# A fused attention, channel-mix and FFT-mix kernel: later output copies and stores, paired value tiles, a third place for weights, a second set of stage buffers, sums apart

## The chip, the cores and the metric

One core of one Trainium2 chip runs the whole program. The metric is the device time of one execution in microseconds (us), median of several runs. A time is also given for the profiled execution, whose trace is quoted below.

## What is computed

Three blocks follow each other: attention with a sigmoid in place of the softmax, a channel mix with token shift (squared ReLU and a sigmoid gate), and a block that adds the real part of a two-dimensional FFT, normalises and runs a two-layer network. All is float32; the kernel multiplies with fp32r operands split into a high and a low part, three matmuls for each product.

```python
# B, S, D = 4, 448, 768; 12 heads of 64
attn = 1 / (1 + exp(-(q @ k.T / 8 - log(S))));  x = attn @ v        # (B, S, D)
xk, xr = mix(x, mu_k), mix(x, mu_r)                                 # with the token before
k = maximum(xk @ w_k, 0);  v = (k * k) @ w_v                        # D -> 1024 -> D
x = sigmoid(xr @ w_r) * v
u = x + real(fft(fft(x, axis=1), axis=2))
un = (u - mean(u)) / sqrt(var(u) + 1e-6)
out = u + maximum(un @ w_ch1, 0) @ w_ch2                            # D -> 3072 -> D
```

## The kernel before

**How the order comes about.** The program is written out by a planner (`Order`, line 136). Each piece of work is a Python generator that yields the planned time at which it wants to go on. `need` (L162) waits until a named mark is set and its planned time has come, `issued` (L169) only until it is set. The planner adds up costs for each engine and for the transfers; an instruction is emitted when its generator comes to it. On the chip each engine then runs its instructions strictly in that order. Matmuls go through a list (`feed`) one at a time. `dma` (L270) puts a transfer on SyncE's queue (SP); with `add=True` it is an accumulation into memory on GpSimd's queue (POOL), and with a third argument `G` a plain transfer on that queue. A delay or a wait in one generator therefore changes where its instructions stand among all others.

**Stages on TensorE.** Attention and keys up to 257 us, receptance (`r`) up to 343, values (`v`, with the FFT's matmuls `pa`, `qa`, `pq` between them) up to 493, the plain part of the first network layer (`f`) up to 562, the visits (`f_X`, `f_Y`, `f_W`) up to 822, the second layer (`m`) to the end. A 448-column matmul takes 0.20 us on the average when nothing waits.

**Values** (`values`, L847). For each of the four batches b six output tiles e are made, each of 8 terms f with 3 matmuls. Term f reads `k2` of (b, f), which `load_k2` (L759) loads into a ring of 12 places: a place is free when the last tile (e = 5) of the batch that used it has read it. `r_t` comes through `load_r` on POOL's queue, and `val_done` (L833) multiplies a tile out of PSUM on VectorE into `x2`, which has three buffers for four batches (`new_x2`, L839, waits for `centre` of batch b - 3). `centre` (L1040) subtracts the mean; for b = 0 it also stores the result to `c_d` on SP. `squares` (L1076) squares the first two batches on ScalarE and stores or accumulates them to `vs_d` on POOL. `rows0` (L1222) forms the sums for the visits after `centre` 1, and `centre` of batch 2 is put in order behind it.

**Visits** (`VISITS`, L131; `visits`, L1318; `visit`, L1377). The first layer is done by a seven-product scheme. Sixteen visits go over groups g of 256 columns: v = 0 to 3 with the first pair of batches (p = 0), v = 4 to 7 with both, v = 8 to 15 with the second (p = 1). A visit for one pair has 63 matmuls. `visit_loads` (L1298) loads two weight chunks for each visit into places `w0`, `w1` (later also `k0` to `k2`), `visits` forms the seven split blocks of them (`blk`), and `after` copies results out of PSUM: `w7` and `u2` (`tmp`, L1381) and stage tiles (`stage`, L1355), all sent to `h_d` on POOL. For p = 0 they lie in buffers `s0`, `s1` and `hst`, for p = 1 in `sum_u`, `sum_v`, `rsb` and `sq`, one of each.

**Second layer** (`second`, L1438). Seven products m for each pair p, 108 matmuls each, three row tiles e side by side. The results gather in three tiles of tag `x2`. For p = 0 `after0` (L1464) scales them, and `store` (L1451) accumulates each into `u_d` and then copies it from there to the output, both on POOL. For p = 1 `after` (L1497) adds onto `u_d` that was loaded, and `store` writes the output by SP.

Of the kernel before, what the change touches and what calls it, by code (L numbers as in the profile page):

```python
# [12 lines left out]
F32 = mybir.dt.float32  # L13
# [8 lines left out]
B, H, S, DH = 4, 12, 448, 64  # L22
D = H * DH
NP = H // 2
DFF = 1024
NF = DFF // 128
# [14 lines left out]
PL, JO, EARLY = 4, 8, 8  # L41
# [239 lines left out]
def build(tc, ap):  # L281
    nc = tc.nc
    V, G = nc.vector, nc.gpsimd
    o = Order(nc)
# [73 lines left out]
    u_d = [dram.tile([128, KD, S], F32, name=f"u_d{b}") for b in range(B)]  # L358
    w0_d = [dram.tile([128, 2, D], F32, name=f"w0_d{f}") for f in range(2 * PL)]
    c_d = dram.tile([128, KD, S], F32, name="c_d")  # L360
# [447 lines left out]
    np_ = pool(s_r, "norm", 1, "right")  # L808
# [38 lines left out]
    def values():  # L847
        for b in range(B):
            o.spawn(new_x2(b))
            for es in ((0,), (1,), (2,), (3,), (4, 5)):  # L850
                while len(o.feed) > 6:
                    yield o.now + 0.1
                ts = [(e, []) for e in es]
                for i in range(0, NF, NF // len(es)):
                    for e, ps in ts:
                        cs = slice(128 * e, 128 * e + 128)

                        def pair(t, b=b, cs=cs):
                            return wvh[:, t, cs], wvl[:, t, cs], k2_t[b, t][:, 0], k2_t[b, t][:, 1]

                        ks = {t: ("k2", b, t) for t in range(NF)}
                        yield from o.tile(
                            partial(bank, f"v_{b}_{e}"),
                            NF,
                            pair,
                            partial(val_done, b, e),
                            ("val", b, e),
                            ks,
                            ps,
                            range(i, i + NF // len(es)),  # L870
                        )
            o.spawn(spectrum(b))
        yield from o.issued(("x2", B - 1, KD - 1))
        o.at["values"] = o.now
# [165 lines left out]
    def centre(b, ps):  # L1040
        u = x2_t[b]
        mean_of = ps[:, 0:S]
        if b < 2:
            o.spawn(squares(b), o.now + 1.0)
        if b == 2:
            yield from o.issued(("centre", 1))
            mean = np_.tile([128, S], F32, tag="rsb", name="mean_2", bufs=1)
            yield o.act(mean, mean_of, AF.Copy, scale=1.0 / D)
        for i in range(3):
            xx = u[:, 2 * i : 2 * i + 2]  # L1050
            yield from o.need(("u_d", b, i))
            for h in range(2):
                if b == 2:
                    t = o.tt(V, xx[:, h], xx[:, h], mean, ALU.subtract)
                else:
                    t = o.stt(xx[:, h], mean_of, -1.0 / D, xx[:, h], ALU.mult, ALU.add)
                o.at["c", b, 2 * i + h] = t
            yield t
            if b == 0:
                o.at["c_d", i] = o.dma(c_d[:, 2 * i : 2 * i + 2], xx) + 2.0  # L1060
            if b < 2:
                continue
            if b > 2 and i == 0:
                yield from o.issued(("scaled", b - 1))
            sq = ft(b, "sq", [128, 2, S], pl=np_)
            yield o.act(sq, xx, AF.Square)
            add_up(b, "v", i, sq)
        if b < 2:
            return
        yield from scale(b)  # L1070
        for i in range(KD):
            t = o.tt(V, u[:, i], u[:, i], rs_t[b], ALU.mult)
            yield t
        o.at["centre", b] = o.now

    def squares(b):  # L1076
        u, landed = x2_t[b], 0.0
        if b > 0:
            yield from o.issued(("centre", 0))
        for i in range(3):  # L1080
            yield from o.need(("c", b, 2 * i + 1))
            if i == 1:
                ts = [np_.tile([128, S], F32, tag=tag, name=f"sq_{b}_{tag}", bufs=1) for tag in ("sum_v", "rsb")]
            else:
                sq = ft(b, "sq", [128, 2, S], pl=np_)
                ts = [sq[:, 0], sq[:, 1]]
            for h, t in enumerate(ts):
                done = o.act(t, u[:, 2 * i + h], AF.Square)
            yield max(done, landed)
            for h, t in enumerate(ts):  # L1090
                landed = o.dma(vs_d[b][:, h], t, G, add=i > 0) + 2.0
            yield landed
        o.at["centre", b] = o.now
# [116 lines left out]
    al = pool(s_l, "al", 1, "left")  # L1210
# [81 lines left out]
    wt_t, place_t = {}, {}  # L1292
    for v, (g, ps) in enumerate(VISITS):
        for j in range(2):
            i = 2 * (v - NG + PL) + j
            place_t[v, j] = ("w0", "w1", "k0", "k1", "k2")[i % 5] if i >= 0 else f"w{j}"

    def visit_loads():  # L1298
        last = {}
        for v, (g, _) in enumerate(VISITS):  # L1300
            for j in range(2):
                place = place_t[v, j]
                if place in last:
                    yield from o.need(("wt free", *last[place]))
                elif place[0] == "k":
                    yield from o.need(("prod", LAST0))
                last[place] = (v, j)
                yield from o.need(("w_d", 2 * g + j))
                name = f"a_{v}_{j}"
                if place in ("w0", "w1"):  # L1310
                    t = al.tile([128, D], F32, tag=place, name=name, bufs=1)
                else:
                    t = ring(23 + 4 * int(place[1]), [128, D], F32, name)
                o.at["wt", v, j] = o.dma(t, w_d[2 * g + j])
                wt_t[v, j] = t
                yield o.now + 0.1
# [36 lines left out]
        yield o.now  # L1353

    def stage(p, q, g):  # L1355
        if p == 0:
            return al.tile([128, S], F32, tag="hst", name=f"h_{p}_{q}_{g}", bufs=2)
        return np_.tile([128, S], F32, tag=("rsb", "sq")[q], name=f"h_{p}_{q}_{g}", bufs=1)

# [3 lines left out]
    def network():  # L1363
# [13 lines left out]
        def visit(v):  # L1377
            g, ps = VISITS[v]
            bk, tm = {}, {}

            def tmp(nm, p):  # L1381
                if p == 0:
                    t = al.tile([128, S], F32, tag={"u2": "s0", "w7": "s1"}[nm], name=f"{nm}_{v}", bufs=1)
                else:
                    t = np_.tile([128, S], F32, tag={"u2": "sum_u", "w7": "sum_v"}[nm], name=f"{nm}_{v}_1", bufs=1)
                tm[nm, p] = t
                return t
# [48 lines left out]
        chain, out = {}, {}  # L1436

        def second(p):  # L1438
# [12 lines left out]
            def store(nm, e, t):  # L1451
                yield t
                b, k = 2 * p + int(nm[1]) - 1, 3 * (int(nm[0]) - 1) + e
                dst = ap["out"][k, :, S * b : S * b + S]
                if p > 0:
                    o.dma(dst, out[p, nm][:, e])
                else:
                    o.dma(u_d[b][:, k], out[p, nm][:, e], add=True)
                    o.dma(dst, u_d[b][:, k], G)

            def add(nm, e, x):
                return o.tt(V, out[p, nm][:, e], out[p, nm][:, e], x, ALU.add)
# [34 lines left out]
            def after(m, e, ps):  # L1497
                if m == 0:
                    if e == 0:
                        tiles("t")  # L1500
                    o.at["tc", p, e] = o.act(out[p, "t"][:, e], ps)
                elif m == 1:
                    if e == 0:
                        tiles("22", "11")
                    yield from o.need(("res", p, "22"))
                    o.at["v", p, e] = add("22", e, ps)
                elif m == 2:
                    yield from store("11", e, add("11", e, ps))
                elif m == 3:
                    if e == 0:  # L1510
                        tiles("12", "21")
                    yield from o.need(("res", p, "12"))
                    o.at["w", p, e] = add("12", e, ps)
                elif m == 4:
                    o.at["z", p, e] = add("22", e, ps)
                elif m == 5:
                    t = out[p, "t"][:, e]
                    yield o.tt(V, t, t, ps, ALU.add)
                    t1, t2 = add("12", e, t), add("22", e, t)
                    o.at["y", p, e] = add("21", e, t)  # L1520
                    yield from store("12", e, t1)
                    yield from store("22", e, t2)
                else:
                    yield from store("21", e, add("21", e, ps))
                yield o.now
# [312 lines left out]
```

## Time and profile before

| | us |
|---|---|
| median of 3 runs (1136.02 to 1138.82) | 1136.56 |
| the profiled execution | 1138.76 |
| its span, first to last instruction | 1137.0 |
| TensorE busy in it | 1120.8 (99%) |
| VectorE busy | 804.3 (71%) |
| ScalarE busy | 649.7 (57%) |
| mean granted clock of TensorE | 0.994 of full speed |

The profile gives the busy time of each engine, the waits, and for any stretch the granted clock. A matmul that runs at half clock is busy twice as long, so a stretch has two losses: the idle time, and its length times what the granted clock lacks to 1.00.

### The profile page before, as it was taken

Reading aid. Unit: us, or ns where it says so; the run is one execution under the profiler, and the core shown is the slowest. Engines: PE = TensorE matmul, PEld = TensorE weight load, DVE = VectorE, ACT = ScalarE, POOL = GpSimd, SP = SyncE. Lnnn points to the kernel's source line nnn. Section 1 sums busy time; section 2 is a strip of 40 time slices with the busy share of each in tenths; the row PEclk is TensorE's granted clock in tenths of the full one; section 3 lists DMA queues with packets and bytes.
Section 4 is the critical chain, followed back from the end, with each engine's and each line's share of the span. In section 5 each row is a group of like instructions: output and inputs, shape, how many; then the busy total and the mean of one; then the engine's idle time right before and its main releaser. Section 6 shows DMA issues by size and latency. Waiting matters only on the chain.

```text
span 1137.0 us, 16897 instructions
## 1 busy us (share of the span) xinstructions
PE 1120.8 (99%) x5908; PEld 977.2 (86%) x5908; DVE 804.3 (71%) x1292; ACT 649.7 (57%) x1171; POOL 108.1 (10%) x205
## 2 busy tenths in 40 slices
PE   9999999999999999999999999999999999989998
PEld 3476676799999989999989999889999999979997
DVE  3876757666624668799787655777579799866887
ACT  6788777766632333354676666767655444444442
POOL 0000000100001011200111112111100100120000
PEclk9999999999999999999999999999999999989999
DMA  7765789768839798855968888989885648974432
GB/s 241 241 232 204 236 315 351 260 234 277 315 133 308 292 324 258 266 154 210 307 220 290 279 289 286 376 296 324 290 335 185 162 155 286 335 200 156 160 99 86
DMA packets 108597, 283.33 MB, mean 249 GB/s; under 512 B 13600, under 2 KB 44512, under 8 KB 108384
## 3 DMA queue, kind: packets, MB, share of 16 engines
q1 hardware_dynamic: 94176, 234.17, 60.5%
q0 software_dynamic: 14048, 47.63, 13.0%
q8 instruction: 46, 0.75, 0.3%
q10 hardware_dynamic: 288, 0.46, 0.1%
q14 instruction: 39, 0.32, 0.1%
HBM read 185.72 MB, written 99.23 MB: 251 GB/s over the span
## 4 chain that ended last, share of the span: by engine, by line
PE 66%; issue 19%; DMA 5%; DVE 4%; POOL 4%; ACT 2%; POOLq 0%; SPq 0%; ACTq 0%; DVEq 0%
PE m L213 20%; PE k L213 9%; PE v L213 9%; PE r L213 8%; PE av L213 6%; PE sc L213 4%; POOL h_d L274 3%; PE f_Y L213 3%; DMA u_d<-out 2%; PE f_W L213 2%; PE f_X L213 2%; PE pq L213 1%; PE sc_c L213 1%; DMA k<-k_d 1%; DVE r L248 1%
## 5 line engine op out<-in xcount | busy, mean ns | idle before, releaser
L213 PE MATMUL m<-hs,sw 128*128 128x448 f32 x1512 | 306.9, 365 | 3.8 <-ACT hs L265 2.9
L213 PEld LDWEIGHTS m<-hs,sw 128*128 128x128 f32 x1512 | 285.7, 189 | 24.6 <-ACT hs L265 3.3
L265 ACT CAST sw<-w 128x768 fp32r<-128x768 f32 x84 | 70.0, 834 | 80.3 <-PE m L213 49.1
L213 PE MATMUL v<-k,wvh 128*128 128x448 f32 x384 | 113.2, 369 | 1.9 <-DMA k<-k_d 1.9
L265 ACT CAST hs<-r 128x896 fp32r<-128x896 f32 x84 | 78.9, 940 | 60.9 <-DVE r L248 60.7
L248 DVE TENSOR_TENSOR sw<-w,sw 128x768 fp32r<-128x768 f32 x84 | 80.1, 954 | 34.0 <-ACT sw L265 33.8
L248 DVE TENSOR_TENSOR hs<-r,hs 128x896 fp32r<-128x896 f32 x84 | 91.3, 1087 | 16.7 <-ACT hs L265 16.4
L267 ACT ACTIVATE sg<-sc,bias_s 128x448 f32<-128x448 f32 x144 | 78.3, 651 | 12.6 <-PE sc L213 12.6
L213 PE MATMUL f_Y<-T,blk 128*128 128x448 f32 x360 | 77.8, 364 | 3.1 <-ACT u L265 3.1
L213 PE MATMUL f_W<-T,blk 128*128 128x448 f32 x360 | 78.4, 366 | 0.0
L213 PEld LDWEIGHTS v<-k,wvh 128*128 128x128 f32 x384 | 71.9, 189 | 7.5 <-DMA k<-k_d 2.6
L213 PEld LDWEIGHTS f_Y<-T,blk 128*128 128x128 f32 x360 | 67.5, 188 | 8.4 <-ACT u L265 3.9
L213 PEld LDWEIGHTS f_W<-T,blk 128*128 128x128 f32 x360 | 68.6, 191 | 4.8
L213 PE MATMUL k<-xkh,wkh 128*128 128x448 f32 x192 | 70.6, 368 | 0.9 <-ACT kt L267 0.9
L213 PE MATMUL k<-xkl,wkh 128*128 128x448 f32 x192 | 70.2, 366 | 0.0
L213 PE MATMUL k<-xkh,wkl 128*128 128x448 f32 x192 | 70.2, 365 | 0.0
L213 PE MATMUL v<-k,wvl 128*128 128x448 f32 x192 | 69.9, 364 | 0.0
L267 ACT ACTIVATE w_raw<-w_raw 128x384 f32<-128x384 f32 x80 | 44.2, 552 | 31.0 <-DMA w_raw<-in_w 31.0
L213 PE MATMUL av<-sg,v 128*64 128x448 f32 x288 | 57.2, 544 | 0.0
L265 ACT CAST blk<-a 128x384 fp32r<-128x384 f32 x80 | 40.5, 511 | 29.0 <-PE f_Y L213 9.8
L213 PE MATMUL f<-un,w1h 128*128 128x448 f32 x192 | 55.5, 364 | 0.0
L248 DVE TENSOR_TENSOR blk<-a,blk 128x384 fp32r<-128x384 f32 x80 | 43.5, 553 | 15.1 <-ACT blk L265 14.9
(227 smaller groups left out, 2146.3 us busy)
## 6 DMA issues: line engine op xcount, KB each, us to landing
w<-v_d SPq DMA_DIRECT2D x84, 384.0 KB, 3.4
w_raw<-in_w SPq DMA_DIRECT2D x80, 384.0 KB, 4.9
r<-h_d SPq DMA_DIRECT2D x48, 448.0 KB, 6.1
k_d<-kp SPq DMA_DIRECT2D x32, 448.0 KB, 3.7
k<-k_d SPq DMA_DIRECT2D x32, 448.0 KB, 6.1
h_d<-h POOLq DMA_DIRECT2D x56, 224.0 KB, 4.6
a<-w_d SPq DMA_DIRECT2D x32, 384.0 KB, 5.6
v_d<-w SPq DMA_DIRECT2D x48, 192.0 KB, 4.5
```

The lines of the kernel that those rows point to most:

```text
L213: self.nc.tensor.matmul(out, lhs, rhs, start=start, stop=stop, skip_group_check=skip)
L248: eng.tensor_tensor(out, a, c, op=op)
L265: self.nc.scalar.copy(out, a)
L267: self.nc.scalar.activation(out, a, fn, **kw)
L274: (eng or self.nc.sync).dma_start(out, src)
```

## The change

- `values`: tiles 0 and 1 of a batch now go in turns of four terms, as 4 and 5 do: half of tile 0, half of tile 1, the rest of 0, the rest of 1.
- `keep`: the stores of `c_d` wait until the last `k2` of batch 2 is planned to have landed; `squares` of batch b waits for the last `k2` of batch b + 2.
- `place_t`, `visit_loads`: the first four visits use the buffer `sq` as a third place for weights, once `centre` of the last batch is over.
- `stage`, `tmp`: odd visits with g below 8 (v = 9, 11, 13, 15) use the buffers of p = 0.
- `store` for p = 0: the copy to the output is issued 15 us after the planned landing of the accumulation. As it is one generator, what stands behind it in `after0` (the sum and the accumulation of "22" behind those of "12") comes later too.
- `after` for p = 1, m = 5: the sum that the last product needs goes first, the other two 2, 7 and 12 us later, one row tile after another.

```diff
@@ values
-            for es in ((0,), (1,), (2,), (3,), (4, 5)):
+            for es in ((0, 1), (2,), (3,), (4, 5)):
@@ centre
             if b == 0:
-                o.at["c_d", i] = o.dma(c_d[:, 2 * i : 2 * i + 2], xx) + 2.0
+                o.spawn(keep(i, xx))
@@
+    def keep(i, xx):
+        yield from o.need(("k2", 2, NF - 1))
+        o.at["c_d", i] = o.dma(c_d[:, 2 * i : 2 * i + 2], xx) + 2.0
+        yield o.now
+
     def squares(b):
         u, landed = x2_t[b], 0.0
+        yield from o.need(("k2", b + 2, NF - 1))
         if b > 0:
@@ place_t
-            place_t[v, j] = ("w0", "w1", "k0", "k1", "k2")[i % 5] if i >= 0 else f"w{j}"
+            k = 2 * v + j
+            place_t[v, j] = ("w0", "w1", "k0", "k1", "k2")[i % 5] if i >= 0 else ("w0", "w1", "w0", "w1", "sq", "w0", "w1", "sq")[k] if k < 8 else f"w{j}"
@@ visit_loads
                     yield from o.need(("wt free", *last[place]))
+                elif place == "sq":
+                    yield from o.need(("centre", B - 1))
...
+                if place == "sq":
+                    t = np_.tile([128, D], F32, tag="sq", name=name, bufs=1)
@@ stage
-        if p == 0:
+        if p == 0 or g < JO and g % 2:
@@ tmp
-                if p == 0:
-                    t = al.tile([128, S], F32, tag={"u2": "s0", "w7": "s1"}[nm], name=f"{nm}_{v}", bufs=1)
+                if p == 0 or g < JO and g % 2:
+                    t = al.tile([128, S], F32, tag={"u2": "s0", "w7": "s1"}[nm], name=f"{nm}_{v}_{p}", bufs=1)
@@ store
-                    o.dma(u_d[b][:, k], out[p, nm][:, e], add=True)
+                    t = o.dma(u_d[b][:, k], out[p, nm][:, e], add=True)
+                    yield t + 15.0
                     o.dma(dst, u_d[b][:, k], G)
@@ after, m == 5
-                    t1, t2 = add("12", e, t), add("22", e, t)
                     o.at["y", p, e] = add("21", e, t)
-                    yield from store("12", e, t1)
-                    yield from store("22", e, t2)
+                    yield o.now + 2.0 + 5.0 * e
+                    yield from store("12", e, add("12", e, t))
+                    yield from store("22", e, add("22", e, t))
```

## Rows read from the trace of the kernel before

**Rows 1.** Page, part 1: busy us of each engine, share, instructions.

```profile
PE 1120.8 (99%) x5908; PEld 977.2 (86%) x5908; DVE 804.3 (71%) x1292; ACT 649.7 (57%) x1171; POOL 108.1 (10%) x205
```

**Rows 2.** TensorE by stretch: width, busy (matmuls), granted clock, DMA share, GB/s.

```profile
415.00:424.00 9.00, 7.05 (x38) 0.81 1.03 416
...
573.00:575.00 2.00, 0.72 (x4) 1.00 0.61 249
...
615.00:616.00 1.00, 0.70 (x4) 1.00 1.16 408
...
736.00:738.00 2.00, 0.79 (x4) 1.00 1.04 408
...
750.00:758.00 8.00, 6.09 (x22) 0.79 0.59 173
...
999.00:1010.00 11.00, 7.68 (x22) 0.69 0.62 125
...
1122.00:1123.00 1.00, 0.53 (x3) 1.00 0.00 0
1123.00:1137.00 14.00, 10.45 (x53) 0.96 0.13 49
```

**Rows 3.** Waits of TensorE: what it waited for, total us, times, longest.

```profile
PE f_Y L213 <- ACT u L265: 3.1, 2, 1.9
PE m L213 <- ACT hs L265: 2.9, 1, 2.9
PE v L213 <- DMA k<-k_d: 1.9, 1, 1.9
PE f_Y L213 <- DVE w L248: 1.3, 1, 1.3
...
PE f_X L213 <- DVE blk L248: 0.3, 1, 0.3
```

**Rows 4.** Chain that ended last: start us, length us, what.

```profile
407.69 9.90 DMA k<-k_d
...
744.88 6.57 DMA h_d<-u
...
822.38 29.04 PE m L213 x145
...
979.30 7.55 DMA u_d<-out
...
996.10 4.26 DMA u_d<-out
```

**Rows 5.** TensorE in the value tiles alone, up to the wait at 415.6 us.

```profile
343.30:415.60 72.30, 65.19 (x309) 1.00 0.87 297
```

**Rows 6.** SyncE in order of time: start, length, instruction.

```profile
407.21 0.38 SPq L274 DMA_DIRECT2D c_d<-x  x1
```

**Rows 7.** GpSimd in order of time, with the idle time before in brackets.

```profile
406.05 1.08 POOL L274 DMA_DIRECT2D vs_d<-sq  x2 [3.42 <-ACT sq L267]
```

**Rows 8.** ScalarE in order of time, idle time before and its releaser in brackets.

```profile
736.74 0.53 ACT L265 COPY u<-f_Y 128x448 f32<-128x448 f32 x1 [0.40 <-DMA h_d<-u]
...
751.52 0.53 ACT L265 COPY u<-f_Y 128x448 f32<-128x448 f32 x1 [2.57 <-DMA h_d<-u]
...
1000.43 1.40 ACT L265 COPY out_t<-m 128x448 f32<-128x448 f32 x3 [10.53 <-DMA u_d<-out]
```

**Rows 9.** VectorE in order of time, likewise.

```profile
483.30 0.62 DVE L248 TENSOR_TENSOR x<-v,rv 128x448 f32<-128x448 f32 x1 [1.56 <-PE v L213]
...
569.79 0.56 DVE L248 TENSOR_TENSOR s<-a,a 128x384 f32<-128x384 f32 x1 [1.00 <-DMA a<-w_d]
...
1002.70 1.09 DVE L248 TENSOR_TENSOR hs<-r,hs 128x896 fp32r<-128x896 f32 x1 [11.81 <-ACT hs L265]
...
1113.44 3.29 DVE L248 TENSOR_TENSOR out<-out,out_t 128x448 f32<-128x448 f32 x6
```

**Rows 10.** All engines by stretch: width, busy PE, PEld, DVE, ACT, POOL, clock.

```profile
500.00:520.00 20.00, 20.00 (x131) 18.86 (x130) 19.00 (x41) 11.08 (x24) 2.72 (x5) 1.00 0.49 160
```

More of the change, by code (lines that the diff above doesn't have):

```diff
@@ L1309, in visit_loads @@
                 name = f"a_{v}_{j}"
-                if place in ("w0", "w1"):
+                if place == "sq":
+                    t = np_.tile([128, D], F32, tag="sq", name=name, bufs=1)
+                elif place in ("w0", "w1"):
                     t = al.tile([128, D], F32, tag=place, name=name, bufs=1)
```

## The prediction, made before the changed kernel was run

> **What bounds the kernel now.** I read the page first: TensorE is busy for 1120.8 of 1137.0 us [rows 1]. So no engine beside it matters on the average, and only two things can be won: the 16.2 us in which it idles, and the time in which it is busy at half clock. The second view is therefore TensorE by stretch, made so that each stretch holds one loss [rows 2]. The reader is to see that nearly all of the idle time after the first 343 us lies in seven short places and in the last 3.5 us, where the last results leave. In three of them the granted clock is below 1.00 as well: it fell to 1.2 GHz after the gap and came back to 2.4 GHz some us later. The loss of a stretch is its width less busy, plus its width times what the clock lacks:
>
> - 415 to 424: 1.95 idle, and 9 x 0.19 = 1.71 by the clock: 3.66 us.
> - 573 to 575: 1.28 us, clock full. 615 to 616: 0.30 us.
> - 736 to 738: 1.21 us. 750 to 758: 1.91 and 8 x 0.21 = 1.68: 3.59 us.
> - 999 to 1010: 3.32 and 11 x 0.31 = 3.41, together 6.73. Counted otherwise: 22 matmuls at 0.20 us would have been 4.4 of 11 us, so 6.6 us. I take 6.6.
> - 1122 to 1123: 0.47 us.
>
> The third view, TensorE's waits [rows 3], names who ended each: a load of k2 (415), the copy of u out of PSUM (736 and 750), the split of hs on ScalarE (1000), a sum on VectorE (573), a weight block (615). Each is then followed back in the chain and in the engines' own order [rows 4, 8, 9].
>
> **Part by part.**
>
> Values. TensorE had done 309 value matmuls when it stopped [rows 5]: 288 of batches 0 and 1 and 21 of tile 0 of batch 2. It stood before term 7, whose k2 was issued at 407.69 and landed 9.90 us later, at 417.6 [rows 4]. Batch 2 had begun 21 x 0.20 = 4.2 us before 415.55, at 411.35. With tiles 0 and 1 in turns, 12 + 12 + 9 = 33 matmuls stand before term 7, so it is wanted at 411.35 + 6.6 = 417.95, after it landed even if nothing else were changed, by a bare 0.35 us. Moving the stores helps more: the c_d store just ahead of that load [rows 6] is 448 KB and the two vs_d stores [rows 7] 448 KB; at the 416 GB/s of this stretch [rows 2] their 0.92 MB take 2.2 us. The load should land near 415.4, 2.5 us before it is wanted. That returns 3.66 us; bounds 0 (the load lands later for another reason) and 3.66. What is moved: three c_d stores on SP and, of each of two batches, six stores on POOL go later. On POOL they stand in the same queue as the loads of r_t, which thereby come no later than before. c_d is read only by loads that wait for tiles of batch 2. The two new waits hold back only their own generators, but behind squares stand centre 0, which frees x2 for batch 3, and centre 1, behind which rows0 and centre 2 stand: several us later, on engines that have time there except VectorE (rivals). I cost that at nothing, covered by TensorE's own row of work; without cover it is the fourth rival.
>
> Weights. The first two visits keep w0 and w1, so the wait at 573, where VectorE stood for 1.00 us before weights of visit 1 at 569.79 [rows 9] and so came late to the sum, is not touched: 0. The loads of visits 2 to 4 can go earlier by about a product (1.8 us) or more, which is over the 0.30 us of 615: 0.30 won, bounds 0 and 0.30 for that place and 1.28 if the order at 573 falls better by chance. The new wait, for centre of the last batch, stands ahead of visit 2's loads only.
>
> Second buffer set. At 736.74 and 751.52 ScalarE wrote u only after the store of the visit before had left its buffer [rows 8]; that store took 6.57 us, from 744.88 to 751.45 [rows 4], and a visit is 63 x 0.20 = 12.6 us long. With two sets in turn each buffer has 12.6 us more than a wait of at most 2.57 us asks for. Both losses go: 1.21 + 3.59 = 4.80 us, and the lower bound is near that. What is late next: nothing within 10 us on this path.
>
> Copies apart. At 1000.43 ScalarE had to write the first tile of the second half and waited for an accumulation into u_d that was issued at 996.10 and landed 4.26 us later [rows 4, 8]. It was so late because POOL issues accumulation, copy, accumulation: each copy waits in the queue for the landing of its own accumulation (7.55 us for the one at 979.30), and the next accumulation waits behind it. Now the accumulations stand in the queue without those copies. The last is "22", e = 2. A product is 108 x 0.2003 = 21.6 us (29.04 us for 145 matmuls [rows 4]); product 5 of the first half ends at 822.4 + 6 x 21.6 = 952.2. After 12 us of spacing and some 1.3 us of sums its "12" is sent at 965.5; the copy follows at the plan's landing (2.9 us by the planner's formula) + 15, at 983.4, and then "22" at about 984.5, landing by 992.1 if it takes the longest 7.55 us. The first tile of the second half is wanted when its product 0 ends, at 822.4 + 8 x 21.6 = 995.4. So the buffer is free 3.3 us early, and whichever of the three buffers is taken is free. TensorE's loss of 6.6 us goes, because it came from ScalarE being 5.0 us late; 1.7 us of lateness was covered by split operands made ahead (3.3 us idle for 5.0 us late). Bounds: 0 and 6.6. The nine copies land later beside loads that are no more than before.
>
> A rule speaks against this part. The accumulation beside which VectorE stood still (for 11.81 us until 1002.70 [rows 9]) landed in 4.26 us, the one at 979.30 in 7.55 us [rows 4]. The Trainium skill, "SBUF — State Buffer", section "SBUF: two separate sides", says that GpSimd can't write the descriptors of its queue's transfers while VectorE runs an operation that holds their shared port (its example is a float32 copy), and the section "A bandwidth-pool intuition that's wrong" gives about 3100 against 620 ns for one transfer. By an estimate from these figures the last accumulation would land 2.5 us later still, at 994.6, 0.8 us before it is wanted: the sum would stay, with a thinner margin for the second rival. The rows agree in direction only; a busier memory around 979 explains them as well.
>
> Sums apart. From 1113.44 VectorE added six results in a row for 3.29 us [rows 9], then three more, and hs came 0.47 us late at 1122 [rows 2]. Six of the nine sums now go behind the first, 2 to 12 us later, between splits: 0.47 won, bounds 0 and 0.47. The last 3.5 us are unchanged: the sums moved are all done before the last product ends, 21.6 us behind product 5.
>
> Against this stands that every engine's order is planned anew from 343 us on. Between 562 and 736 the present plan left two small waits that nobody meant, 1.28 and 0.30; I take one more of their mean, 0.8 us; bounds 0 and a wait like that of 1000, 6.6.
>
> Sum: 3.66 + 0.30 + 4.80 + 6.60 + 0.47 = 15.8, less 0.8, so 15.0 us. The profiled execution took 1138.76 (span 1137.0 and 1.76 around it) and would take 1123.7. It is 2.2 us above the median of the runs, 1136.56; I carry the difference over: **1121.5 us**.
>
> **The rivals.**
>
> First, the values' gain is swallowed by VectorE. It last waited for TensorE at 483.30 [rows 9] and is busy for 19.00 of 20 us at 500 to 520 [rows 10], while TensorE waits for nothing. For it: hardly any slack. Against: its work there is released by TensorE's own results and moves forward with them. Price 3.66: 1125.2 us.
>
> Second, the buffer at 995 isn't free in time: "22" slips over 5 us (3.3 of margin and 1.7 of cover). For it: the change itself puts "22" some 18 us behind "12", and VectorE is full there. Against: the order before had the same accumulation issued at 996.10, 11 us after the time planned now. Price 6.6: 1128.1 us.
>
> Third, the change moves waits rather than removes them: the large ones go, and the new plan leaves others of the same kind, two of 6.6, as a buffer or a landing that the planner costs too low. Against: buffers only become more. Result 1134.7 us.
>
> Fourth, slower: VectorE becomes the bound at 483 to 530. Squares of batch 1 start only behind the last k2 of batch 3, so rows0 (21 operations of 0.62 us, as the row at 483.30) and centre 2 with its sums (11 such) come as one block, 32 x 0.62 = 19.8 us, ahead of the FFT operands of batch 3 that TensorE needs. If none of it were hidden, that and a clock loss as at 1000 (3.4) cost 23.2 us: 1144.8 us. It turns the sign only from 15.0 us of uncovered block on, and TensorE has the plain products to do meanwhile.
>
> **How the numbers follow.** Chances: forecast 0.60, first rival 0.14, second 0.12, third 0.08, fourth 0.06. A measurement of this kernel can tell about 0.3% (3.4 us) from no change. Faster by more: 0.60 + 0.14 + 0.12 = 0.86; within: 0.08; slower: 0.06. The range reaches from all terms without new waits and with 573 gone as well (1136.56 - 15.8 - 1.28 = 1119.4, and 0.9 for the spread of runs) to the second rival with another wait of 1.28: 1118.5 to 1129.5.
>
> **What would show it.** Right: no TensorE wait for k and clock 1.00 around 412 to 420; no wait of u for h_d between 715 and 755; ScalarE writes out_t with no wait for u_d; nine accumulations on POOL with no copy between the first ones; TensorE idle near 8 us in all. Wrong: an idle TensorE with VectorE full at 480 to 530, or the wait at 1000 there again, or a new wait of some us in the visits.

## The result and the profile after

The changed kernel takes **1123.49 us** (median of four runs, 1123.17 to 1123.58). The kernel before, four runs beside it, takes 1137.61 us (1136.02 to 1138.82). The ratio is 0.9876, with a 95% interval of 0.9859 to 0.9893. The forecast was 1121.5 us. The profiled execution of the changed kernel took 1123.54 us with a span of 1121.8 us, where the profiled one of before took 1138.76 and 1137.0.

First the line of TensorE on the page, its busy time, share and instructions, beside [rows 1]; then its waits, beside [rows 3].

```profile
PE 1112.6 (99%) x5908; PEld 972.7 (87%) x5908; DVE 804.0 (72%) x1292; ACT 648.1 (58%) x1171; POOL 107.6 (10%) x205
```

```profile
PE f_Y L213 <- ACT u L265: 3.3, 2, 1.7
PE k L213 <- ACT kt L267: 0.9, 3, 0.5
PE warm L658 <- DVE bias_s L388: 0.9, 1, 0.9
PE f_Y L213 <- DVE w L248: 0.3, 1, 0.3
```

The reader is to see two things. TensorE idles for 9.2 us of the span instead of 16.2, and none of the waits that the prediction named is left at its place: no load of k, no hs, no weight block, no u in the late visits. Instead there are two waits for u that the kernel before did not have. TensorE by stretch shows where (width, busy, granted clock, DMA share, GB/s), beside [rows 2]:

```profile
343.00:493.00 150.00, 150.00 (x872) 1.00 0.85 282
...
577.00:580.00 3.00, 1.30 (x7) 1.00 0.79 304
580.00:592.00 12.00, 12.00 (x61) 1.00 0.50 166
592.00:595.00 3.00, 1.42 (x8) 1.00 0.92 295
...
724.00:725.00 1.00, 0.66 (x4) 1.00 1.03 398
725.00:1118.00 393.00, 393.00 (x1965) 1.00 0.68 230
```

The losses are 1.70, 1.58 and 0.34 us, all before 725, and from there to 1118 TensorE is busy without a gap. The granted clock is 1.00 in each of these stretches, so the half-clock stretches of [rows 2], which cost some 6.8 us of before, are gone as well.

By stages, from the first instruction of each on TensorE, the changed profile is 4.70 us ahead at the first visit (it begins at 557.58 instead of 562.28), gains 2.98 us more in the visits (the second layer begins at 814.54 instead of 822.22) and 7.52 us in the second layer: 15.2 us of span. The prediction's terms give 3.66, 4.3 (4.80 + 0.30 - 0.80) and 7.07, together 15.0. Of the 4.70 us, 0.60 are there before the first value matmul (342.57 instead of 343.17), in a stretch that no part of the change touches; the value stage itself took 146.26 us instead of 150.28.

The new waits come from ScalarE, which writes u only once the store of the visit before has left its buffer (ScalarE's rows, with the idle time before each and what ended it):

```profile
575.21 0.53 ACT L265 COPY w<-f_W 128x448 f32<-128x448 f32 x1 [1.75 <-DMA h_d<-w]
...
578.94 0.53 ACT L265 COPY u<-f_Y 128x448 f32<-128x448 f32 x1 [1.91 <-DMA h_d<-u]
...
593.62 0.53 ACT L265 COPY u<-f_Y 128x448 f32<-128x448 f32 x1 [3.98 <-DMA h_d<-u]
```

These are the wait of [rows 8], now in the early visits (half 0 alone), which the change left with one set of buffers.

The second layer, GpSimd's queue from 950 us on (L272 issues an accumulation, L274 a copy):

```profile
950.10 0.90 POOL L272 DMA_DIRECT2D u_d<-out  x1 [56.97 <-DVE out L248]
954.04 0.86 POOL L272 DMA_DIRECT2D u_d<-out  x1 [3.04 <-DVE out L248]
957.97 0.84 POOL L272 DMA_DIRECT2D u_d<-out  x1 [3.07 <-DVE out L248]
969.31 1.72 POOL L272 DMA_DIRECT2D u_d<-out  x2 [10.49 <-DVE out L248]
970.39 1.19 POOL L274 DMA_DIRECT2D out<-u_d  x1
...
981.34 0.85 POOL L272 DMA_DIRECT2D u_d<-out  x1 [2.00 <-DVE out L248]
981.88 2.42 POOL L274 DMA_DIRECT2D out<-u_d  x4
986.78 0.53 POOL L274 DMA_DIRECT2D out<-u_d  x1 [2.48 <-DMA u_d<-out]
990.24 0.53 POOL L274 DMA_DIRECT2D out<-u_d  x1 [2.93 <-DMA u_d<-out]
```

Five accumulations stand before the first copy, and the last of the nine goes out at 981.34. It lands at about 990.2, which releases its copy. ScalarE writes the first tile of the second half before that, waiting for nothing but TensorE:

```profile
987.34 1.14 ACT L265 COPY out_t<-m 128x448 f32<-128x448 f32 x2 [0.76 <-PE m L213]
```

### The profile page after: what moved, and what is told of

It reads as the page before. It is cut to its first block, busy times and chain, and to the rows that moved or that the text cites. A ratio compares the mean times of both kernels' runs of the same rounds, so it can differ in the third digit from the quotient of the medians.

```text
span 1121.8 us, 16880 instructions
## 1 busy us (share of the span) xinstructions
PE 1112.6 (99%) x5908; PEld 972.7 (87%) x5908; DVE 804.0 (72%) x1292; ACT 648.1 (58%) x1171; POOL 107.6 (10%) x205
## 4 chain that ended last, share of the span: by engine, by line
PE 95%; issue 1%; DMA 1%; ACT 1%; DVE 0%; POOL 0%; SPq 0%; POOLq 0%; ACTq 0%; DVEq 0%
PE m L213 27%; PE v L213 10%; PE k L213 10%; PE f_Y L213 8%; PE r L213 8%; PE av L213 6%; PE f_W L213 6%; PE f_X L213 6%; PE f L213 5%; PE sc L213 5%; PE pq L213 1%; PE sc_c L213 1%; PE pa L213 1%; PE qa L213 1%; DMA a<-w_d 1%
## 5 line engine op out<-in xcount | busy, mean ns | idle before, releaser
L213 PE MATMUL m<-hs,sw 128*128 128x448 f32 x1512 | 303.2, 362 | 0.0
```

Source lines behind the costliest of these rows:

```text
L213: self.nc.tensor.matmul(out, lhs, rhs, start=start, stop=stop, skip_group_check=skip)
```

## The experiments

They ran in three groups. In each the kernel before ran beside them on the same chip: 1133.41 us (1131.17 to 1136.29), 1134.95 (1129.69 to 1136.60) and 1135.12 (1130.36 to 1138.54). Each edit is against the changed kernel, save in the second.

| kernel | edit | us (lowest to highest) |
|---|---|---|
| copies_back | copies behind accumulations again | 1128.78 (1125.44 to 1130.79) |
| one_set | no second buffer set | 1126.02 (1125.52 to 1126.93) |
| values_back | both parts at the values undone | 1124.87 (1124.39 to 1127.34) |
| early_set | second set in early visits too | 1120.03 (1119.73 to 1120.72) |
| after_again | none | 1123.83 (1122.89 to 1124.15) |
| no_pairs | value tiles one by one | 1124.52 (1123.61 to 1125.08) |
| stores_back | stores ahead of loads of k | 1124.97 (1123.79 to 1125.28) |
| no_third | no third place for weights | 1123.16 (1122.46 to 1124.67) |
| copies_only | before, copies apart alone | 1128.54 (1127.16 to 1131.87) |
| late_buffer | out_t in the buffer of "22" | 1123.26 (1123.20 to 1123.65) |
| early_no_third | early_set, no third place | 1122.40 (1121.76 to 1123.14) |
| sums_back | sums together again | 1124.13 (1123.49 to 1128.13) |

### The copies of u_d

**One part undone.**

```diff
-                    t = o.dma(u_d[b][:, k], out[p, nm][:, e], add=True)
-                    yield t + 15.0
+                    o.dma(u_d[b][:, k], out[p, nm][:, e], add=True)
```

> The changed kernel, with one part undone: each copy of u_d to the output is issued right behind its accumulation again (no 15 us between). My theory: the copies again hold GpSimd's queue up, the last accumulation goes out near 996 to 1000 less the 8 us by which this stage now comes earlier (so near 988 to 992), and the first tile of the second half waits for it: TensorE loses about 6.6 us, 1130 us, with ScalarE's first out_t waiting for the write into u_d. Rival: what helped is only that the planner gave the second half's first tile another buffer; then the wait stays away whether the copies stand between or not: 1123 to 1124 us.

1128.78 us: 5.3 us back in the median, 6.3 in the span of the profiled execution (1128.1). The runs spread with the clock: 1125.44 and 1126.47 us at a mean granted clock of 1.000 and 0.999, 1128.40 to 1130.79 at 0.998 and 0.997. GpSimd's queue and ScalarE's row in it:

```profile
979.41 0.89 POOL L272 DMA_DIRECT2D u_d<-out  x1
987.27 0.56 POOL L274 DMA_DIRECT2D out<-u_d  x1 [6.97 <-DMA u_d<-out]
987.82 0.90 POOL L272 DMA_DIRECT2D u_d<-out  x1
992.50 0.56 POOL L274 DMA_DIRECT2D out<-u_d  x1 [3.78 <-DMA u_d<-out]
```

```profile
992.28 1.40 ACT L265 COPY out_t<-m 128x448 f32<-128x448 f32 x3 [10.48 <-DMA u_d<-out]
```

This is [rows 4, 8] again: the copy stands 6.97 us in the queue for the landing of its own accumulation, the accumulation behind it goes out at 987.82, and ScalarE waits 10.48 us for it. TensorE then stood for 2.87 and 0.39 us, and behind that the clock was 0.50:

```profile
991.00:994.60 3.60, 0.73 (x5) 0.99 0.34 77
994.60:1001.00 6.40, 6.01 (x15) 0.50 0.72 146
```

**The same part alone, in the kernel before.**

```diff
-                    o.dma(u_d[b][:, k], out[p, nm][:, e], add=True)
+                    t = o.dma(u_d[b][:, k], out[p, nm][:, e], add=True)
+                    yield t + 15.0
```

> The kernel before with one part of the change alone: the nine copies of u_d to the output are issued 15 us behind their accumulations. Theory: in the kernel before the loss near 1000 was 6.6 us; undoing this part in the changed kernel brought 5 to 6 us back (1128.78 against 1123.5 us, with single runs from 1125.4 to 1130.8), so the part alone gives 5 to 6.6 us: a ratio of 0.9942 to 0.9956 to the kernel before, and no wait of the first out_t of the second half for u_d. Rival: in the kernel before, whose accumulations start 8 us later, beside other transfers, they land later still and the first tile waits for them in spite of the order: a ratio of 0.997 to 1.000.

The ratio to the kernel before is 0.9943 (0.9919 to 0.9967), 6.6 us less (1135.12 to 1128.54): the whole of the prediction's 6.6 us. TensorE has no gap there (30.00 us busy in 980 to 1010, clock 1.00), and the other waits of before stand where they stood. The second layer alone took 308.01 us instead of 314.78 here, and 313.97 instead of 307.26 with the copies back: 6.8 and 6.7 us. So the theory holds in both directions.

**Which buffer.** The prediction held that whichever of the three buffers is taken is free. That is not what the rows after show: out_t was written at 987.34, and the accumulation out of "22", e = 2 landed at 990.2. It did no harm, because out_t of the second half had been given the buffer of "12" and "21", not that of "22" and "11" as before: the buffers are taken in the order in which the plan frees them, and the copies' place changes that order. The other buffer with the copies in between wasn't run. In copies_back the three accumulations of "21" are the last ones (993.04, 998.23 and 1004.04 us), so that buffer would have come free later than the one that ScalarE waited for. This edit puts out_t into the old buffer while the copies stay apart:

```diff
                 if m == 0:
                     if e == 0:
+                        tiles("12", "21")
+                        tiles("22", "11")
                         tiles("t")
```

(The two later places that made these tiles are taken out.)

> The changed kernel with the tiles of the second half taken in another order, so that its first tile (out_t) goes into the buffer of "22" and "11" of the first half, as in the kernel before; in the changed kernel it went into that of "12" and "21". The prediction held that whichever of the three buffers is taken is free. In the changed kernel the last accumulation out of "22" was issued at 981.34 us and landed at 990.2 us, ScalarE wrote out_t at 987.34 us. Theory: out_t waits 2.9 us, of which operands split ahead cover 1.7 us, so TensorE loses 1.2 us, with the clock up to 2.5 us: 1124.7 to 1126 us. Rival (the prediction's): the accumulation is in time or covered, 1123.5 us.

ScalarE did wait, and TensorE did not:

```profile
988.69 0.97 ACT L265 COPY out_t<-m 128x448 f32<-128x448 f32 x2 [2.49 <-DMA u_d<-out]
```

```profile
980.00:1010.00 30.00, 30.00 (x151) 1.00 0.94 348
```

This execution runs some 0.35 us ahead of the changed kernel's here (its last accumulation goes out at 981.00 instead of 981.34), so out_t came about 1.7 us late (988.69 less 986.99), and TensorE is busy for all 30 us. The time is 1123.26 us, not my 1124.7 to 1126. So 1.7 us of lateness is covered, as the prediction worked out from before (5.0 us late, 3.3 us idle), and the choice of buffer decides nothing here. But the 3.3 us by which the prediction had the buffer free early do not exist in the old buffer; the cover alone carries it.

### The second buffer set

```diff
     def stage(p, q, g):
-        if p == 0 or g < JO and g % 2:
+        if p == 0:
...
             def tmp(nm, p):
-                if p == 0 or g < JO and g % 2:
+                if p == 0:
```

> The changed kernel, with one part undone: every visit of half 0 uses the one set of buffers again (stage and tmp). My theory: the copy of u out of PSUM waits again for the store of the visit before in the late visits (715 to 755), which costs 4.8 us, split 1.2 and 3.6 with the clock: about 1128.3 us. Rival: the two waits went because the stores land sooner at another place of the plan; then no wait of that kind returns, 1123.5 us.

1126.02 us, 2.2 to 2.5 us more than the changed kernel, where I had expected 4.8. The two waits come back at their places (TensorE's rows), but shorter than in [rows 2]:

```profile
733.62 2.07 PE L213 MATMUL f_Y<-T,blk 128*128 128x448 f32 x9 [1.12 <-ACT u L265]
...
747.57 2.08 PE L213 MATMUL f_Y<-T,blk 128*128 128x448 f32 x9 [0.88 <-ACT u L265]
```

The clock stayed at 1.00. The early waits for u are shorter in this profile than in the changed kernel's (0.68 and 1.25 us instead of 1.70 and 1.58), so TensorE's waits in the visits grew by 0.9 us only (4.48 instead of 3.62), while the visits took 2.25 us longer (259.21 instead of 256.96); the rest is not traced to a wait. In copies_only, whose visits are those of before, the same two gaps are 1.20 and 1.00 us, again with the clock at 1.00. The 3.59 us of the second place in the profile of before (1.91 idle and the clock) was thus the price in that execution, not the usual one.

**The set in the early visits too.** The changed kernel's largest loss is the same wait in visits 1 and 2, so the second and the fourth early visit take the other set for u2 and w7 (the names of the tiles are told apart as well):

```diff
-                if p == 0 or g < JO and g % 2:
+                if p == 0 and (g >= JO or g % 2 == 0) or p > 0 and g < JO and g % 2:
```

> The changed kernel with one thing more: the second and fourth of the four early visits (half 0 alone) take the other set for u2 and w7 (the buffers sum_u and sum_v), as the late visits do by turns. My theory: the two waits of the changed kernel in which ScalarE's copy of u stands behind the store of the visit before (1.91 and 3.98 us on ScalarE at 578.9 and 593.6, 1.70 and 1.58 us of TensorE) both go: 1120.2 us. Rival: the loads and sums around them are late too, and the wait moves to the weight block or the sum behind it: 1122 to 1123.5 us.

**1120.03 us**, 3.5 us under the changed kernel's 1123.49 and 3.8 under its 1123.83 (both measured in other groups), and the fastest of all kernels here. All of TensorE's waits in it:

```profile
PE warm L658 <- DVE bias_s L388: 0.9, 1, 0.9
PE k L213 <- ACT kt L267: 0.9, 3, 0.5
PE f_Y L213 <- DVE w_n L248: 0.2, 1, 0.2
PE sc L213 <- DMA q<-in_q: 0.2, 1, 0.2
```

Of the waits in the visits 0.2 us is left. Those for u could be removed by themselves; nothing came in their place.

### The values

**Both parts undone** (es one by one, c_d stored at once, squares without their wait):

```diff
-            for es in ((0, 1), (2,), (3,), (4, 5)):
+            for es in ((0,), (1,), (2,), (3,), (4, 5)):
...
-                o.spawn(keep(i, xx))
+                o.at["c_d", i] = o.dma(c_d[:, 2 * i : 2 * i + 2], xx) + 2.0
...
-        yield from o.need(("k2", b + 2, NF - 1))
```

> The changed kernel, with both parts at the value products undone: tiles 0 and 1 one behind the other, and the stores of c_d and vs_d ahead of the loads of k again. My theory: TensorE waits again 1.95 us for k2 near 415, the clock falls, 3.7 to 4.5 us are lost: 1127.2 to 1128.0 us. Rival (the gain is swallowed by VectorE): 1123.5 to 1124.5 us, with VectorE's later waits gone instead.

1124.87 us: 1.0 to 1.4 us more, not 3.7 to 4.5. The wait is there, at the place of [rows 3]:

```profile
417.04 0.68 PE L213 MATMUL v<-k,wvh 128*128 128x448 f32 x2 [1.40 <-DMA k<-k_d]
```

It is 1.40 us long and the clock stays at 1.00 behind it. In copies_only the same wait was 2.28 us, with a granted clock of 0.87 over the 10 us from 418 on; in the profile of before 1.95 us and 0.81 [rows 2]. The rest of the difference is that this plan meets the visits otherwise: no wait for u at 577 and 592, but 1.23 us at 572 and 0.87 at 586 for the sum w on VectorE, the wait that [rows 2] show at 573, and 1.22 at 728 for a weight block. TensorE's waits from 343 us on add up to 4.72 us here and to 3.62 in the changed kernel.

**Each part by itself.** With the first line of the diff above alone:

> The changed kernel with the value tiles one behind the other again, but the stores of c_d and vs_d still behind the loads of k. By the steps of the prediction: the load of k2 that was late lands near 415.4 and term 7 of tile 0 is wanted at 411.35 + 4.2 = 415.55, so the stores alone hide it by 0.15 us: no loss, within 0.5 us of the changed kernel. Rival: the load lands later than that (the two of batch 2 before it and the loads of r_t share the memory) and the pairs are what hides it: a wait of 0.5 to 1.5 us for k on TensorE and as much more in the time.

With the other two alone:

> The changed kernel with the stores of c_d and vs_d ahead of the loads of k again, but with tiles 0 and 1 in turns. By the steps of the prediction the pairs alone hide the load by a bare 0.35 us: no wait for k or one under 0.3 us, within 0.5 us of the changed kernel. Rival: both parts are needed; then a wait for k near 418 of some 0.5 to 1.5 us.

1124.52 and 1124.97 us beside 1123.83: 0.7 and 1.1 us, with ranges that overlap. Neither has a wait for k near 415 to 420. So either part is enough there, as the prediction's 0.15 and 0.35 us had it. But they aren't the same elsewhere. Without the pairs the next batch meets the wait:

```profile
455.65 0.67 PE L213 MATMUL v<-k,wvh 128*128 128x448 f32 x2 [1.15 <-DMA k<-k_d]
```

Without the stores moved there is none, but TensorE waits for VectorE further on, at 495 (0.85 and 0.19 us, un) and 533 (0.41, sum_u). Only together do they leave the stage free of waits. Both kernels also wait 1.30 and 1.12 us for a weight block at 728, which the changed kernel does not, so 0.7 and 1.1 us are not the price of the value stage alone.

### The third place for weights

```diff
-  ... if i >= 0 else ("w0", "w1", "w0", "w1", "sq", "w0", "w1", "sq")[k] if k < 8 else f"w{j}"
+  ... if i >= 0 else f"w{j}"
```

> The changed kernel with the weights of the four early visits in two places again (w0, w1). The changed kernel lost 1.70 and 1.58 us near 577 and 592 where ScalarE's copy of u waited for the store of the visit before, which the kernel before did not. Theory: with the third place the blocks and the products of visits 1 and 2 come earlier, and so the one buffer set of the early visits is wanted earlier than its store has landed; without it the two waits for u shrink or go, and a wait for a weight block or sum (0.3 and 1.3 us in the kernel before) comes back: 1121.5 to 1123.5 us, so the third place is worth nothing or less. Rival: the place does gain; then waits for weight blocks of 1 to 3 us come back beside the waits for u: 1124.5 to 1126.5 us.

1123.16 us against 1123.83: no difference that shows. In its trace the two waits for u are one of 0.74 us, and two for weight blocks are there (0.52 and 0.30 us). SyncE's loads of weights show what the place does, in the changed kernel and without it:

```profile
560.25 0.32 SPq L274 DMA_DIRECT2D a<-w_d  x1
562.28 0.32 SPq L274 DMA_DIRECT2D a<-w_d  x1
571.43 0.32 SPq L274 DMA_DIRECT2D a<-w_d  x1
```

```profile
559.72 0.32 SPq L274 DMA_DIRECT2D a<-w_d  x1
570.90 0.32 SPq L274 DMA_DIRECT2D a<-w_d  x1
```

One load goes out at 562.28 that otherwise waits until 570.90 for a place. So the place did what the prediction paid it 0.30 for. That TensorE, being earlier, then runs into the one buffer set is the likely reason why nothing is gained: its waits for u are 2.50 us in after_again and 0.74 here. To see the place's worth with that out of the way, the same edit was made in early_set:

> The changed kernel with the second set of buffers in the early visits too (1120.03 us in an earlier group), and the weights of these visits in two places again. The third place gave nothing in the changed kernel (1123.83 us with it, 1123.16 us without, on one chip), and my theory is that the waits for u hid its worth. Theory: with those gone the place pays its 0.3 to 1.3 us: 1120.3 to 1121.5 us here, with TensorE waiting for weight blocks or sums at 570 to 620. Rival: it is worth nothing here either: 1120.0 us, no such waits.

1122.40 us against 1120.03 (on another chip). TensorE waits 0.70 us for w and 0.42 and 0.95 us for weight blocks, 2.07 us in all, where early_set has 0.2. The waits account for 1.9 of the 2.4 us; it is more than the 0.3 to 1.3 us that I had expected. The place is worth about 2 us, which the changed kernel doesn't get.

### The sums, and the kernel itself again

```diff
-                    o.at["y", p, e] = add("21", e, t)
-                    yield o.now + 2.0 + 5.0 * e
-                    yield from store("12", e, add("12", e, t))
-                    yield from store("22", e, add("22", e, t))
+                    t1, t2 = add("12", e, t), add("22", e, t)
+                    o.at["y", p, e] = add("21", e, t)
+                    yield from store("12", e, t1)
+                    yield from store("22", e, t2)
```

> The changed kernel with one part undone: the three sums behind product 5 of the second half stand together again. Theory: hs comes late again before the last product, 0.47 us on TensorE (1122 to 1123 in the kernel before), 1124.0 us against 1123.5. Rival: the last product's operands come earlier by the other parts of the plan and nothing is lost: 1123.5 us, no wait for hs after 1090.

1124.13 us, 0.3 to 0.6 more, which the times alone (1123.49 to 1128.13) don't tell from nothing. The trace does: the wait of [rows 2] at 1122 is back in its old size, 0.47 there and 0.48 here:

```profile
1108.16 10.89 PE L213 MATMUL m<-hs,sw 128*128 128x448 f32 x53 [0.48 <-DVE hs L248]
```

> The changed kernel itself, unaltered, beside the others of this group on one chip. In the group before, the kernel before took 1133.41 us where it took 1137.61 us beside the first profile of the changed kernel, so differences of 2 us between kernels are only read within one group. Theory: the changed kernel is bound by TensorE almost everywhere and has few landings that it waits for, so it moves less between chips than the kernel before: 1122 to 1124 us. Rival: all kernels move alike by the chip, then 1119 to 1120 us where the kernel before takes 1133.

1123.83 us where the kernel before took 1134.95, and 1123.49 where it took 1137.61: the first theory. The changed kernel's eight runs lie within 1.3 us. Those of before lie within 9.1 us (1129.69 to 1138.82), and their time goes with the mean granted clock: in the three groups the runs at 0.995 took 1134.92 to 1138.54 us, those at 0.998 took 1131.17 to 1134.51, and the single one at 1.000 took 1129.69. The gain therefore depends on which runs of before it is held against: the ratio is 0.9911 (0.9882 to 0.9939) in this group and 0.9876 in the first comparison. Against that single run at 1.000 it is about 6 us (1129.69 to 1123.83), not 11 to 14, so about half of the gain seems to be clock that is no longer lost.

## Why the prediction was right, and where it wasn't

The forecast of 1121.5 us lay 2.0 us under the measured time; it is inside the range of 1118.5 to 1129.5. The gain was forecast as 15.0 us from the median and measured as 14.1 in the first comparison and 11.1 beside after_again. The signs that the prediction named for being right all showed, save that TensorE idles for 9.2 us where it said near 8; one sign for being wrong showed as well, a new wait of some us in the visits. Step by step:

**The sum agreed, in part by luck; what was done with it was wrong.** Profile against profile the prediction says 1123.7 us and 1123.54 was measured. But the errors cancel: against the terms the value stage gave 0.4 us more, the visits 1.3 less, the second layer 0.5 more, and 0.6 came from ahead of all that. The last step carried over the 2.2 us by which the profiled execution of before lay above the median. That is the 2.0 us. It assumed that an execution's excess stays when its cause is removed. The excess was most likely in the very waits that the change takes away; no trace of a quicker execution of before was kept that would show it. Undone singly, those waits cost 1.0 to 1.4 us (values) and 2.2 to 2.5 us (buffer set), where the profile of before showed 3.66 and 4.80. Most of the difference is clock, 1.71 and 1.68 us in that profile and nothing in these two, and the time of before goes with the clock from run to run (after_again). After the change the profiled execution lay 0.05 us above its median.

**Values.** Mechanism right (no wait for k, clock 1.00), and both of the bare margins bore out at 415. The stage gave 4.02 us between the two profiles (150.28 to 146.26) instead of 3.66; where the other 0.4 us come from the rows don't show. What the step left out is that the next batch has the same wait in store, 1.15 us at 455 with the stores moved alone.

**Weights, and the allowance for new waits.** This step failed in its sizes. 0.30 us was won, as said; the 1.28 us at 573, costed at 0, went as well; and the allowance of 0.8 us for a new wait was 3.62 us (1.70, 1.58, 0.34), 3.22 in after_again. The prediction wrote of the second buffer set that nothing is late next within 10 us. It looked at the late visits alone. The early visits have one set as well, and there the third place makes TensorE earlier: no_third and early_set show the two sides. Together the terms of the visits were 1.3 us too high.

**Second buffer set.** Mechanism right: no wait of u in the late visits after, two with the set undone. Undone it cost 2.2 to 2.5 us, not 4.80; in copies_only the two waits are 2.20 us, with the clock at 1.00.

**Copies apart.** Right in mechanism and size: 6.6 forecast, 6.6 alone, 5.3 undone. But the working that had the buffer free 3.3 us early was off. From the start of the second layer the last "22" was to go out after 162.1 us (984.5 less 822.4) and to land after 169.7; it went out after 166.8, behind VectorE's sum, and landed after 175.7, while the tile was wanted after 172.8, as forecast (173.0). So 4.7 of the 6.0 us of slip are in the sending. The other 1.3 are in the landing: it took 8.9 us, where the step put 7.55 as the longest. Already in the trace of before the nine took 4.3 to 8.2 us; in the changed kernel they took 4.4, 8.2 and 9.7 (lowest, median, highest). That it cost nothing was luck of the plan, which had given the tile another buffer. In the old buffer the cover of 1.7 us was enough, as late_buffer showed. The rule that the prediction weighed (the Trainium skill, "SBUF — State Buffer", "SBUF: two separate sides", with the times of "A bandwidth-pool intuition that's wrong") would by its estimate have put the landing 2.5 us later than the forecast's. The last accumulation took 1.3 us longer than the 7.55 us, so the trace agrees in direction. But VectorE's rows from 960 to 982 us in the changed kernel are all TENSOR_TENSOR, not the copy of the rule's example, and no run changed VectorE's load, so none shows that this is why.

**Sums apart.** Right: 0.47 forecast, 0.48 us of TensorE when undone.

**The rivals.** VectorE swallowing the values' gain: not so, TensorE is fully busy from 343 to 493 and on to the visits; a shadow of it is seen only with the stores back (1.45 us of waits for un and sum_u). The buffer late at 995: its condition, a slip of over 5 us, came true in the changed kernel (6.0 us), but in a buffer that the tile did not need; with the old buffer forced the tile came 1.7 us late, and that was covered. Waits moved: yes in kind, 3.6 us instead of 13.2. The block on VectorE: no trace of it.

## What to carry to other kernels

A profiled execution is one draw. Where a wait's length wavers and the clock falls only behind the longer ones, the loss read from one profile is that draw's price: sum against the profile, and do not carry its distance from the median over to a kernel from which the wavering waits are gone. When a resource is doubled at one place because a store outlasts a turn, look for every other place that still has one, above all where the same change lets work come earlier; here that was worth 3.5 us more. And in a queue that waits, a transfer that depends on the one just ahead of it is put behind all that do not: nine copies moved back, no work saved, 6.6 us.

## What the runs showed of the hardware

Accumulations into DRAM from GpSimd's queue landed later each when they went out closer together: the nine took 8.2, 7.6 and 8.1 us in the median (changed kernel, late_buffer, copies_only) against 5.9 and 5.5 us with a wait for each between them (before, copies_back). In stretches of 10 us from 945 to 995 the share of the DMA engines was 0.65 to 1.07 in these five. The nine were through sooner all the same: the last was issued at 981.3 instead of 1013.1 us.

TensorE's clock stayed at 2.4 GHz behind gaps of 0.88, 1.12, 1.40, 1.58 and 1.70 us, and was at 1.2 GHz for a while behind gaps of 1.91, 1.95, 2.28, 2.87 and 2.92 us (the last is the longer of the two gaps in the 3.32 us of [rows 2] at 999). That is all that these runs show of it; what TensorE did between the gaps differed as well. It makes the same wait cost 1.4 us in one execution (values_back) and 3.7 in another (before, [rows 2]). copies_only is a second case of the dearer kind:

```profile
415.00:418.00 3.00, 1.60 (x9) 1.00 1.03 419
418.00:428.00 10.00, 10.00 (x75) 1.00 1.05 364
```

```profile
415.00:418.00 3.00, 0.72 (x3) 0.85 1.02 415
418.00:428.00 10.00, 10.00 (x69) 0.87 1.05 376
```

The first two lines are values_back (1.40 us of wait), the other two copies_only (2.28 us), TensorE by stretch. In the same 10 busy us the second passed 6 matmuls fewer.
